# Last token tile: five PSUM banks in turn for its MoE, expert weights split in pieces of 1024 columns, its rows' scale from the bits of the norm on VectorE

## The chip, the cores and the metric

The kernel runs on one core of one Trainium2 chip. The metric is device time in microseconds (us) of one execution, lower is better. Names of engines are those of the profile: PE is TensorE (PEld its weight loads), DVE is VectorE, ACT is ScalarE, POOL is GpSimd, SP is SyncE. "Lo" and "hi" are the two float16 halves into which the kernel splits every float32 matrix so that three float16 products replace one float32 product.

## The reference

Three layers follow one another on 1152 tokens of 512 values.

```
attn:  2 batches x 8 heads x 576 x 64, top_k = 32 of 576 scores kept, softmax, times v
x      = attn as (1152, 512)
moe:   xn = x / sqrt(mean(x*x) + 1e-6) * rms_g
       x  = (silu(xn @ w_gate) * (xn @ w_val)) @ w_out          # 512 -> 1536 -> 512
moe2:  expert = argmax(x @ r_gate, 8 experts); gate_w = softmax of the same logits at that expert
       disp[e, c] = x[i]   in order of i, at most 288 rows for an expert
       y   = relu(disp @ w1[e]) @ w2[e]                         # 512 -> 1024 -> 512
       out[i] = gate_w[i] * y[expert[i], pos[i]]
```

## The kernel before

The 1152 tokens are nine tiles of 128 rows (t = 0 to 8). For each tile, attention runs over four pairs of heads; after it come `norm(t)`, `moe1(t)` (the dense MoE) and `dispatch(t)` (routing, and one indirect DMA that writes the tile's rows to `disp` in HBM). A table of slots (`at(...)`) says when each of these generators takes a step, and a scheduler orders the instructions of each engine from that; the order that results is fixed when the kernel is built. Attention is the largest part of the span (until about 511 us); what follows it is the subject here: tile 7's MoE is half done then, tile 8's MoE still has to run alone, and then the eight experts.

`moe1(t)` has six products `b` = 0 to 5 of twelve matmuls each (128x512), gate and value in turn for three groups g of 512 columns. Each fills one PSUM bank `a` of the pool `pm` (three banks). For tile 8, ACT takes the tanh of a gate product (`th`), DVE makes the gate from it (L456) and multiplies the value product by it (L459, `gs`); only then is a bank free. `turned(g)` transposes the result on PE, also through `pm`, and ACT and DVE make its halves `hT` (L422, L423). The 36 matmuls of the second layer (L473) add up in `yps`, also a bank of `pm`, and ACT copies it out as `yx` (L479).

`dispatch(t)` takes the norm of the rows on ACT (L495), a power of two near its inverse square root on POOL (`pow`, L132 and L133, called from L497) and DVE (L139, L142), scales the rows, finds the expert, and DVE writes the row numbers into `slot` (L554). POOL then issues the scatter (L556). For tile 8 the first gather, of expert 0's first 128 rows ("a"), is issued on ACT's queue (L760, L773) and waits for tile 7's scatter. After tile 8's scatter SP issues the gathers of experts 1 to 3, and of the rest of expert 0 ("b": POOL fetches its rows as `xb`, SP transposes them).

The sixteen expert weights (`w1`, `w2` of eight experts, 2 MB each, loaded as two DMAs of 1 MB) come in the order `ORDER`; below, weight n is the n-th in that order. Each passes through `load` (SP's queue), `size` (two ACT squares of 2048 columns into `junk`, L720, a small PE sum, five small DVE steps) and `convert` (hi half on ACT L744 and on DVE L746, lo half in two DVE pieces L749). Weights 0 and 1 are read from the buffers `split2` and `split3`, the others from `raw` buffers, of which there are two at first and four in the expert stage. A raw buffer is free when its weight's lo half is done. Weights 0 to 3 are sized and converted during tile 8's MoE, weight 4 at its end, weights 5 to 15 in the expert stage. The loads of weights 5, 6 and 7 are issued only after the gather of expert 3 (`issue_after(last.ins)`).

In the expert stage PE alternates `up` and `down` (L832), 96 matmuls each; `up` of expert e needs weight `w1[e]` converted.

## Time and profile before

| | us |
|---|---|
| median of 3 runs | 720.37 (718.26 to 722.33) |
| the profiled execution, device time | 719.72 |
| its span, first to last instruction | 717.9 |
| busy: PE / DVE / ACT / POOL | 557.7 / 625.8 / 493.6 / 423.4 |
| mean granted TensorE clock | 0.933 |

The profile is of one execution; 1.8 us lie around its span. A time such as 571.45 is counted from the span's start. A share of busy time over the whole span says little here, since attention, the dense MoE and the experts have different limits; what counts is who waits for whom after 511 us.

### The profile page before, as it was taken

The page shows a single profiled execution, that of the slowest core. Times are in us where ns is not written, and L with a number is a line of the kernel's source. Part 1 is how long each engine was busy: PE and PEld are TensorE (multiplying, and loading weights), DVE is VectorE, ACT ScalarE, POOL GpSimd, SP SyncE. Part 2 cuts the span into 40 slices and gives each one's busy share as a digit, 9 for nine tenths or more (in the row PEclk, how much of TensorE's full clock was granted, in tenths as well). Part 3 has the DMA queues.
Part 4 walks back from the last instruction along what each step waited for, and adds up shares of the span by engine and source line. Part 5 has one row for each costly group of instructions (what it writes and reads, how often), then busy time and mean ns, then how long its engine had stood idle before and what let it go on. Part 6 is the DMA issues. An engine that isn't in the chain of part 4 may idle for free.

```text
span 717.9 us, 12959 instructions
## 1 busy us (share of the span) xinstructions
PE 557.7 (78%) x4700; PEld 400.0 (56%) x4700; DVE 625.8 (87%) x1296; ACT 493.6 (69%) x939; POOL 423.4 (59%) x446
## 2 busy tenths in 40 slices
PE   1216425476667999999999999998987859999995
PEld 1115314334344666666556565665534549998994
DVE  3999999999999999999999999997389534989960
ACT  3456447559957788878688778877797317998811
POOL 3786888867895778866858767765513220023412
PEclk9999655569999999999999999999999989999998
DMA  8999161385000002000000000000933179999101
GB/s 212 270 320 288 43 211 38 125 248 166 8 8 16 16 22 50 27 12 16 23 16 24 16 15 16 1 16 1 370 114 118 45 203 362 296 328 296 44 21 38
DMA packets 47016, 80.00 MB, mean 111 GB/s; under 512 B 18732, under 2 KB 23340, under 8 KB 46946
## 3 DMA queue, kind: packets, MB, share of 16 engines
q1 hardware_dynamic: 43954, 74.02, 33.7%
q0 software_dynamic: 1792, 4.83, 1.8%
q8 instruction: 39, 0.64, 0.4%
q10 hardware_dynamic: 1200, 0.26, 0.2%
q14 instruction: 31, 0.25, 0.1%
HBM read 64.35 MB, written 12.27 MB: 107 GB/s over the span
## 4 chain that ended last, share of the span: by engine, by line
DVE 49%; issue 15%; PE 11%; ACT 8%; DMA 8%; POOL 6%; SPq 1%; POOLq 0%; ACTq 0%; DVEq 0%
DVE r L333 14%; DVE m L336 14%; DVE m L324 5%; PE pm L448 4%; PE pm L473 3%; DMA raw<-in_w_dram 3%; DVE wbig L157 3%; DMA wbig<-in_w_out_dram 3%; ACT junk L720 2%; DVE wbig L159 2%; DVE wbig L228 2%; POOL out_dram L874 2%; DMA vt<-in_v_l_dram 2%; DVE split L749 1%; DVE hT L423 1%
## 5 line engine op out<-in xcount | busy, mean ns | idle before, releaser
L448 PE MATMUL pm<-wbig,xn 128*128 128x512 f16 x648 | 165.3, 390 | 10.4 <-POOL wbig L225 3.2
L336 DVE MAX8 m<-r 128x8 f32<-128x576 f32 x216 | 157.1, 747 | 0.3
L832 PEld LDWEIGHTS <-split 128*128 128x128 f16 x1728 | 115.2, 99 | 13.1 <-issue 13.0
L310 PE MATMUL tp<-kst,qh 128*128 128x288 f32 (+1 forms) x160 | 64.8, 416 | 64.6 <-ACT s L312 23.8
L353 POOL TENSOR_TENSOR pp<-s,pp 128x576 f32<-128x576 f32 x72 | 102.7, 1442 | 8.6 <-ACT pp L352 8.4
L333 DVE MATCH_REPLACE8 r<-m,r 128x576 f32<-128x576 f32 x144 | 106.5, 742 | 0.0
L448 PEld LDWEIGHTS <-xn 128*128 128x128 f16 x648 | 62.9, 100 | 74.6 <-issue 16.2
L473 PE MATMUL pm<-wbig,hT 128*128 128x512 f16 x324 | 80.9, 388 | 11.9 <-POOL wbig L229 3.1
L310 PEld LDWEIGHTS tp<-kst,qh 128*128 128x128 f32 (+1 forms) x160 | 32.3, 203 | 92.2 <-ACT s L312 31.8
L352 ACT ACTIVATE pp<-s,bias 128x576 f32<-128x576 f32 x72 | 52.0, 773 | 27.9 <-POOL bias L338 27.6
L376 PE MATMUL tp<-ident,pp 128*128 128x128 f32 x324 | 57.9, 295 | 15.8 <-ACT pp L358 7.3
L312 ACT ACTIVATE s<-tp 128x288 f32<-128x288 f32 x144 | 54.8, 412 | 19.3 <-POOL pp L353 15.8
L874 POOL DMA_INDIRECT out_dram<-ob,tos x14 | 23.1, 1647 | 73.8 <-ACT ob L872 71.7
L749 DVE SCALAR_TENSOR_TENSOR split<-raw,sc,split 128x2048 f16<-128x2048 f32 x28 | 65.1, 2344 | 0.3 <-ACT split L744 0.3
L832 PE MATMUL acc<-hE,split 128*128 128x168 f16 (+2 forms) x864 | 58.7, 228 | 2.9 <-DVE hE L843 2.0
L384 PE MATMUL xps<-pt,vt 128*64 128x128 f32 (+1 forms) x800 | 57.9, 284 | 2.9 <-ACT pt L377 2.9
L377 ACT ACTIVATE pt<-tp 128x384 f32<-128x384 f32 x108 | 49.3, 494 | 14.1 <-PE tp L376 11.4
L376 PEld LDWEIGHTS tp<-ident,pp 128*128 128x128 f32 x324 | 41.7, 150 | 30.5 <-ACT pp L358 10.1
L720 ACT ACTIVATE junk<-raw 128x2048 bf16<-128x2048 f32 x28 | 53.4, 1909 | 7.4 <-DMA raw<-in_w_dram 7.2
L832 PE MATMUL acc<-xgT,split 128*128 128x168 f16 (+1 forms) x768 | 56.6, 234 | 2.3 <-DVE yT L851 2.3
L358 ACT ACTIVATE pp<-pp,bias 128x576 f32<-128x576 f32 x72 | 56.4, 785 | 0.1
L473 PEld LDWEIGHTS <-hT 128*128 128x128 f16 x324 | 30.4, 100 | 45.7 <-issue 11.8
(191 smaller groups left out, 1247.3 us busy)
## 6 DMA issues: line engine op xcount, KB each, us to landing
raw<-in_w_dram SPq DMA_DIRECT2D x28, 1024.0 KB, 7.9
wbig<-in_w_out_dram SPq DMA_DIRECT2D x6, 1024.0 KB, 9.9
disp<-wraw SPq DMA_DIRECT2D x18, 257.0 KB, 7.0
qraw<-in_q_l_dram SPq DMA_DIRECT2D x72, 64.0 KB, 2.2
wraw<-in_w_gate_dram SPq DMA_DIRECT2D x8, 512.0 KB, 4.5
split<-in_w_dram SPq DMA_DIRECT2D x4, 1024.0 KB, 7.2
kraw<-in_k_l_dram SPq DMA_DIRECT2D x12, 288.0 KB, 4.3
wbig<-in_w_val_dram SPq DMA_DIRECT2D x3, 1024.0 KB, 6.1
```

What stands on the lines that cost most here:

```text
L310: nc.tensor.matmul(sp[:c1], x[:, i, :c1], kst[b, hp][:, i, c * HALF:(c + 1) * HALF], start=(n == 0), stop=(n == 1))
L333: nc.vector.match_replace(r[i], m[:, i, n - 1], src, -3.0e38)
L336: nc.vector.max(m[:, i, n], r[i])
L353: nc.gpsimd.tensor_tensor(w, s[i], w, op=OP.subtract)
L358: nc.scalar.activation(pp[p][:, i], pp[p][:, i], AF.Exp, bias=bias[:, i, 0:1], scale=0.125, accum_out=sums[t][:, h:h + 1])
L376: nc.tensor.transpose(tp[:, i, :], p2[:, o:o + P], ident)
L384: nc.tensor.matmul(xps[t][rows, hp, c0:c1], v, w, start=(n == 0), stop=(n == 4))
L448: nc.tensor.matmul(a, xn[:, x + c, :], half(i, lo), start=(c == 0 and n == 0), stop=(c == KC - 1 and n == 2))
L473: nc.tensor.matmul(yps, hT[f // KC][:, KC * hi + f % KC, :], half(i, lo), start=(f == 0 and n == 0), stop=(f == NF1 - 1 and n == 2))
L720: nc.scalar.activation(junk, raw[:, g * BIG:(g + 1) * BIG], AF.Square, accum_out=sc[:, 9 + g:10 + g])
L749: nc.vector.scalar_tensor_tensor(lo[:, r], raw[:, r], sc[:, 7:8], hi[:, r], op0=OP.mult, op1=OP.subtract)
L832: nc.tensor.matmul(a, u[:, c, col * P:(col + 1) * P], v[:, c, :a.shape[-1]], start=(c == 0 and n == 0), stop=(c == nk - 1 and n == 2))
```

## The change

Four edits, all for what follows attention. First, when attention's PSUM is given back, a new pool `late` takes two of its banks, and tile 8's products b = 1, 2, 4, 5 use them; b = 0 and 3, the transposes and `yps` stay in `pm`. Tile 8's `moe1` starts at table slot 18 of its stretch and not 12, which is after the pool is made. Second, weights 0 to 3 are squared and converted in four pieces of 1024 columns and not two of 2048 (the first half on ACT, the second on DVE, as before); weights 4 to 15 keep two pieces. Third, tile 8's power of two is worked out on DVE from the bits of the norm, as the expert weights' already is, and POOL's two steps go. Fourth, as a result, the scheduler orders all engines anew from tile 8's MoE on.

```diff
--- before.py
+++ after.py
@@ -424,6 +424,8 @@
 
     yx = {}
 
+    late = []
+
     def moe1(t, ew):
         hT = [mx.tile([P, 2 * KC, P], F16, name="hT", bufs=3) for _ in range(3)]
         xn = xnT.pop(t)
@@ -440,8 +442,8 @@
             if ew is nc.gpsimd:
                 gs = mx.tile([P, DM], F32, name="gs")
             for w in range(2):
-                a = pm.tile([P, DM], F32, name="pm")
                 b = 2 * g + w
+                a = late[0].tile([P, DM], F32, name="late") if late and b % 3 else pm.tile([P, DM], F32, name="pm")
                 for c in range(KC):
                     i = KC * b + c
                     for n, (x, lo) in enumerate(((0, 0), (0, 1), (KC, 0))):
@@ -493,8 +495,8 @@
         nc.gpsimd.tensor_copy(yd[:, DM + 1:ROW], tok[:, t:t + 1])
         yn = route.tile([P, 8], F32, name="yn")
         nc.scalar.activation(yd[:, :DM // 2].bitcast(BF16), y, AF.Square, accum_out=yn[:, 0:1])
-        size = pow2_below_rsqrt(yn[:, 1:2], yn[:, 2:3], yn[:, 0:1], 1.01, yn[:, 3:5])
-        next(size)
+        size = iter(()) if t == NT - 1 else pow2_below_rsqrt(yn[:, 1:2], yn[:, 2:3], yn[:, 0:1], 1.01, yn[:, 3:5])
+        next(size, None)
         yield
         lp = px.tile([P, 3, E], F32, name="px")
         for c in range(KC):
@@ -504,6 +506,13 @@
         nc.vector.tensor_copy(lg, lp[:, 0, :])
         for _ in size:
             pass
+        if t == NT - 1:
+            nc.vector.tensor_scalar(yn[:, 3:4], yn[:, 0:1], 1.1, TINY, op0=OP.mult, op1=OP.add)
+            bits = yn[:, 4:5].bitcast(I32)
+            nc.vector.tensor_scalar(bits, yn[:, 3:4].bitcast(I32), 1, 0x7fff0000, op0=OP.logical_shift_right, op1=OP.bitwise_and)
+            nc.vector.tensor_scalar(bits, bits, -1, 0x5f370000, op0=OP.mult, op1=OP.add)
+            exponent(yn[:, 1:2], yn[:, 4:5])
+            invert(yn[:, 2:3], yn[:, 1:2])
         nc.vector.tensor_scalar(yn[:, 5:6], yn[:, 1:2], YS, None, op0=OP.mult)
         if t == NT - 1:
             nc.scalar.activation(yh, y, AF.Copy, scale=yn[:, 5:6])
@@ -646,7 +655,7 @@
         ew = nc.vector if t in (0, 8) else nc.gpsimd
         t0 = (4 * t + 5) * SL
         at(t0 + 1, ahead(norm(t, ew), 300), 1)
-        at(t0 + 12, ahead(moe1(t, ew), 0), 2.7)
+        at(t0 + (12 if t < NT - 1 else 18), ahead(moe1(t, ew), 0), 2.7)
         at(t0 + 10 + 4 * SL, ahead(dispatch(t), 0), 3 if t < NT - 1 else 1)
     live = []
     slot = 0
@@ -675,6 +684,7 @@
     ps.release()
     ew = ctx.enter_context(tc.tile_pool(name="ew", bufs=1, reuse_waits="tile"))
     pst = ctx.enter_context(tc.tile_pool(name="pst", bufs=1, space=PSUM, side="right", reuse_waits="tile"))
+    late.append(tc.alloc_tile_pool(name="late", bufs=2, space=PSUM, side="right"))
     slots = [ew.tile([P, 8 * DM], F32, name=f"split{i}") for i in range(4)]
     raws = [ew.tile([P, 8 * DM], F32, name=f"raw{i}") for i in range(2)]
     es = {}
@@ -715,14 +725,15 @@
         e, w = divmod(j, 2)
         raw = raw_of(n)
         sc = ew.tile([P, 13], F32, name="sc", bufs=8)
-        for g in range(2):
-            junk = ew.tile([P, BIG], BF16, name="junk")
-            nc.scalar.activation(junk, raw[:, g * BIG:(g + 1) * BIG], AF.Square, accum_out=sc[:, 9 + g:10 + g])
+        k = 4 if n < 4 else 2
+        for g in range(k):
+            junk = ew.tile([P, BIG], BF16, name="junk")[:, :2 * BIG // k]
+            nc.scalar.activation(junk, raw[:, g * 2 * BIG // k:(g + 1) * 2 * BIG // k], AF.Square, accum_out=sc[:, 9 + g:10 + g])
         t = pst.tile([P, DM], F32, name="st")
-        s16 = ew.tile([P, 2], BF16, name="s16", bufs=2)
-        nc.vector.tensor_copy(s16, sc[:, 9:11])
-        for g in range(2):
-            nc.tensor.matmul(t[:, 0:1], ones16, s16[:, g:g + 1], start=(g == 0), stop=(g == 1))
+        s16 = ew.tile([P, 4], BF16, name="s16", bufs=2)
+        nc.vector.tensor_copy(s16[:, :k], sc[:, 9:9 + k])
+        for g in range(k):
+            nc.tensor.matmul(t[:, 0:1], ones16, s16[:, g:g + 1], start=(g == 0), stop=(g == k - 1))
         nc.vector.tensor_scalar(sc[:, 2:3], t[:, 0:1], 1.01, TINY, op0=OP.mult, op1=OP.add)
         half_bits = sc[:, 3:4].bitcast(I32)
         nc.vector.tensor_scalar(half_bits, sc[:, 2:3].bitcast(I32), 1, 0x7fff0000, op0=OP.logical_shift_right, op1=OP.bitwise_and)
@@ -738,14 +749,15 @@
     def convert(j, n):
 
         raw, (hi, lo), sc = raw_of(n), place(j), sized.pop(j)
-        for g in range(2):
-            r = slice(g * BIG, (g + 1) * BIG)
-            if g == 0:
+        k = 4 if n < 4 else 2
+        for g in range(k):
+            r = slice(g * 2 * BIG // k, (g + 1) * 2 * BIG // k)
+            if 2 * g < k:
                 nc.scalar.activation(hi[:, r], raw[:, r], AF.Copy, scale=sc[:, 7:8])
             else:
                 nc.vector.tensor_scalar(hi[:, r], raw[:, r], sc[:, 7:8], None, op0=OP.mult)
-        for g in range(2):
-            r = slice(g * BIG, (g + 1) * BIG)
+        for g in range(k):
+            r = slice(g * 2 * BIG // k, (g + 1) * 2 * BIG // k)
             nc.vector.scalar_tensor_tensor(lo[:, r], raw[:, r], sc[:, 7:8], hi[:, r], op0=OP.mult, op1=OP.subtract)
 
     meta, every, xgT, hE, yT2 = {}, {}, {}, {}, {}
@@ -788,6 +800,7 @@
         fetch_w()
     while live or fill:
         advance()
+    late.pop().release()
     px.release()
     pm.release()
     wts.release()
```

The new order is shown at three places. Line numbers of the changed kernel are its own: L457 to L461 there are L455 to L459 before, L731 is L720, L756 is L744, L758 is L746, L761 is L749, L718 is L708.

DVE before, from the third weight's hi half to tile 8's last gate (`th` is a gate, `gs` a value product, `sc` the small steps of a weight's size, `split` with a number is a weight's converted buffer):

```order
L746 TENSOR_SCALAR split_5660<-raw_5662,sc 128x2048
L527 MAX k_5704<-key 128x8
L735 TENSOR_TENSOR sc<-sc 128x1
L749 SCALAR_TENSOR_TENSOR split_5660<-raw_5662,sc,split_5660 128x2048
L530 TENSOR_SCALAR oh<-rank_72,k_5704 128x8
L749 SCALAR_TENSOR_TENSOR split_5660<-raw_5662,sc,split_5660 128x2048
L539 TENSOR_SCALAR nm<-nm 128x1
L456 SCALAR_TENSOR_TENSOR th<-th,pm 128x512
L538 SCALAR_TENSOR_TENSOR scr,pos<-first,oh 128x8
```

DVE of the change, from tile 8's last gate to its last `hT`:

```order
L458 SCALAR_TENSOR_TENSOR th<-th,late 128x512
L739 TENSOR_SCALAR sc<-sc 128x1
L423 TENSOR_TENSOR hT<-pm,hT 128x512
L461 SCALAR_TENSOR_TENSOR gs<-late,st,th 128x512
...
L761 SCALAR_TENSOR_TENSOR split_5636<-raw_5638,sc,split_5636 128x1024 x2
L739 TENSOR_SCALAR sc<-sc 128x1
L761 SCALAR_TENSOR_TENSOR split_5636<-raw_5638,sc,split_5636 128x1024
L548 TENSOR_SCALAR nm<-nm 128x1
L539 TENSOR_SCALAR oh<-rank_72,k_5684 128x8
L423 TENSOR_TENSOR hT<-pm,hT 128x512
```

Before, the last gate stood behind the whole conversion of weights 2 and 3 (`split_5660` is weight 3's); now it stands ahead of both, and the last `hT` stands behind weight 2's (`split_5636`).

ACT before, around the copy of tile 8's result `yx`:

```order
L720 ACTIVATE junk,sc<-raw_5661 128x2048
L760 DMA_TRANSPOSE xgT<-disp 128x8x128
L773 DMA notes_5885<-disp 128x2
L422 ACTIVATE hT<-pm 128x512
L479 ACTIVATE yx<-pm,st 128x512
L744 ACTIVATE split_5988<-raw_5661,sc 128x2048
L495 ACTIVATE yd,yn<-yx 128x512
```

ACT of the change, the same place:

```order
L481 ACTIVATE yx<-pm,st 128x512
L731 ACTIVATE junk,sc<-raw_5638 128x2048
L492 ACTIVATE xu<-px 128x512
L772 DMA_TRANSPOSE xgT<-disp 128x8x128
L785 DMA notes_5889<-disp 128x2
L497 ACTIVATE yd,yn<-yx 128x512
L731 ACTIVATE junk,sc<-raw_5638 128x2048
```

The gather "a" and its notes moved from ahead of `yx` to between `yx` and tile 8's norm (L497), and weight 4's squares (`raw_5638`) moved behind `yx`.

SP before, its DMAs from weight 4's load on (each row is one weight's two DMAs; `raw_5661` twice is weights 4 and 8, `raw_5662`, `raw_5989` and `raw_5990` below the gathers are weights 5, 6, 7):

```order
L708 DMA raw_5661<-in_w_dram 128x2x1024 x2
L708 DMA raw_5661<-in_w_dram 128x4x512 x2
L760 DMA_TRANSPOSE xgT<-disp 128x8x176
...
L760 DMA_TRANSPOSE xgT<-disp 128x8x176
L708 DMA raw_5662<-in_w_dram 128x2x1024 x2
L708 DMA raw_5989<-in_w_dram 128x4x512 x2
L708 DMA raw_5990<-in_w_dram 128x2x1024 x2
```

SP of the change:

```order
L718 DMA raw_5638<-in_w_dram 128x2x1024 x2
L772 DMA_TRANSPOSE xgT<-disp 128x8x176
...
L772 DMA_TRANSPOSE xgT<-disp 128x8x176
L718 DMA raw_5639<-in_w_dram 128x2x1024 x2
L718 DMA raw_6034<-in_w_dram 128x4x512 x2
L718 DMA raw_6035<-in_w_dram 128x2x1024 x2
L718 DMA raw_5638<-in_w_dram 128x4x512 x2
```

Weight 8's load moved from ahead of the gathers to behind weight 7's load, and with it weight 4's conversion, which frees its buffer: on DVE that now stands behind tile 8's scatter.

## Rows read from the trace of the kernel before

**Rows 1.** Windows: length; busy us of PE, PEld, DVE, ACT, POOL; clock; DMA share; GB/s.
```profile
526.00:568.00 42.00, 33.50 (x157) 15.69 (x155) 33.27 (x67) 27.26 (x34) 7.72 (x8) 0.92 0.19 64
580.00:600.00 20.00, 12.48 (x224) 12.22 (x222) 2.98 (x10) 3.66 (x5) 2.40 (x3) 0.83 0.84 237
600.00:710.00 110.00, 104.31 (x1454) 101.67 (x1451) 87.52 (x140) 79.13 (x88) 22.07 (x13) 1.00 0.66 197
```

**Rows 2.** Timeline of PE in tile 8's MoE: start, us, instruction, [idle before <-releaser].
```profile
529.67 4.02 PE L448 MATMUL pm<-wbig,xn 128*128 128x512 f16 x10
...
539.66 2.75 PE L448 MATMUL pm<-wbig,xn 128*128 128x512 f16 x12 [1.19 <-DVE th L456]
...
548.19 2.75 PE L448 MATMUL pm<-wbig,xn 128*128 128x512 f16 x12 [1.44 <-DVE th L456]
...
556.69 7.03 PE L473 MATMUL pm<-wbig,hT 128*128 128x512 f16 x24 [2.69 <-DVE th L456]
```

**Rows 3.** Timeline of ACT and DVE in the same stretch.
```profile
528.36 0.60 ACT L422 ACTIVATE hT<-pm 128x512 f16<-128x512 f32 x1
...
531.86 0.69 DVE L423 TENSOR_TENSOR hT<-pm,hT 128x512 f16<-128x512 f32 x1
...
557.40 0.73 DVE L459 SCALAR_TENSOR_TENSOR gs<-pm,st,th 128x512 f32<-128x512 f32 x1
```

**Rows 4.** Timeline: tile 8's result, norm, power of two and slots.
```profile
568.17 0.69 ACT L479 ACTIVATE yx<-pm,st 128x512 f32<-128x512 f32 x1 [3.27 <-PE pm L473]
...
570.65 0.62 ACT L495 ACTIVATE yd<-yx 128x512 bf16<-128x512 f32 x1
...
571.98 2.56 POOL L133 TENSOR_TENSOR yn<-yn,mhalf 128x1 f32<-128x1 f32 x1
...
574.57 0.15 DVE L139 TENSOR_SCALAR yn<-yn 128x1 int32<-128x1 int32 x1 [0.47 <-POOL yn L133]
...
578.38 0.15 DVE L554 TENSOR_TENSOR slot<-pos 128x1 int32<-128x1 f32 x1
```

**Rows 5.** Timeline: tile 7's slots, scatter, and the gather "a" on ACT's queue.
```profile
558.37 0.16 DVE L554 TENSOR_TENSOR slot<-pos 128x1 int32<-128x1 f32 x1
...
562.26 1.36 ACTq L760 DMA_TRANSPOSE xgT<-disp  x1
...
563.65 0.60 ACTq L773 DMA_DIRECT2D notes<-disp  x1
```

**Rows 6.** Chain of waits behind tile 8's scatter: start, us, what.
```profile
583.16 4.99 DMA xb<-disp,rest
```

**Rows 7.** Timeline: loads on SP's queue, and PE's first matmul behind the gathers.
```profile
571.90 2.59 SPq L708 DMA_DIRECT2D raw<-in_w_dram  x2
...
590.90 6.56 SPq L708 DMA_DIRECT2D raw<-in_w_dram  x6
591.06 4.00 PE L832 MATMUL acc<-xbT,split 128*128 128x48 f16 x96 [6.68 <-DMA xbT<-xb]
```

**Rows 8.** Timeline: weight 4's lo half on DVE, a later load, the last lo half.
```profile
569.49 4.61 DVE L749 SCALAR_TENSOR_TENSOR split<-raw,sc,split 128x2048 f16<-128x2048 f32 x2
...
610.53 2.03 SPq L708 DMA_DIRECT2D raw<-in_w_dram  x2
...
685.75 4.61 DVE L749 SCALAR_TENSOR_TENSOR split<-raw,sc,split 128x2048 f16<-128x2048 f32 x2
```

**Rows 9.** The page's groups for a weight's lo piece and square: busy, mean ns.
```profile
L749 DVE SCALAR_TENSOR_TENSOR split<-raw,sc,split 128x2048 f16<-128x2048 f32 x28 | 65.1, 2344 | 0.3 <-ACT split L744 0.3
...
L720 ACT ACTIVATE junk<-raw 128x2048 bf16<-128x2048 f32 x28 | 53.4, 1909 | 7.4 <-DMA raw<-in_w_dram 7.2
```

**Rows 10.** Timeline: two of POOL's scatters of results, and DVE beside the first.
```profile
630.65 2.34 DVE L749 SCALAR_TENSOR_TENSOR split<-raw,sc,split 128x2048 f16<-128x2048 f32 x1
...
631.05 2.80 POOL L874 DMA_INDIRECT out_dram<-ob,tos  x1 [15.55 <-ACT ob L872]
...
695.43 0.93 POOL L874 DMA_INDIRECT out_dram<-ob,tos  x1 [0.30 <-issue]
```

## The prediction

> **What bounds the kernel now.** The change touches nothing ahead of tile 8's MoE, so I read the windows behind attention first. The windows [rows 1] show three stretches. In 526 to 568, tile 8's MoE runs alone: PE is busy 33.5 of 42 us, and part of that at the lower of its two clock levels (granted 0.92 of 2.4 GHz on the mean). In 580 to 600, between tile 8's scatter and the experts, every engine idles: DVE is busy 3.0 of 20 us, ACT 3.7. In 600 to 710 PE is busy 104.3 of 110 us at full clock, DVE 87.5, ACT 79.1: the experts run at PE's pace. So the end moves with the moment at which PE may start on the gathered rows, 591.06, where it had waited 6.68 us for the last transposed gather [rows 7]. The chain of waits shows what stands there: the fetch of `xb`, 4.99 us, behind tile 8's scatter [rows 6]. The scatter follows `slot`, which DVE writes at 578.38 [rows 4]. Hence the question is how much earlier `slot` comes.
>
> Back from `slot`, PE's timeline [rows 2] shows tile 8's MoE waiting for a PSUM bank three times, 1.19, 1.44 and 2.69 us, each time for DVE's gate (L456), and ten matmuls at 0.40 us each (4.02 us) where twelve later ones took 2.75, that is 0.22. The last gate was late because DVE had two weights to convert first; the last `gs` came at 557.40 [rows 3]. The result was copied out at 568.17 and its norm taken at 570.65; POOL's `pow` then took 2.56 us, and DVE could go on at 574.57 [rows 4].
>
> **The change, step by step.** A price first. A piece of 1024 columns does not occur before. A lo piece lies between half of 2.34 [rows 9], 1.17, and a third of the way from 0.69 for 512 columns [rows 3] to 2.34, which is 1.24; I take 1.22. A square lies between half of 1.91 and a third of the way from 0.62 [rows 4] to 1.91, 0.95 to 1.05; I take 1.05. Four weights have eight squares and four hi pieces more on ACT, and four hi and eight lo pieces more on DVE, each at most 0.19 and 0.14 dearer: at most 2.3 us on ACT and 1.7 on DVE over 45 us, nothing below. They count where the engine is the bound.
>
> 1. *Start.* Tile 7's `hT` on ACT was at 528.36 [rows 3], behind four squares of 2048 columns and a hi half. Now six squares of 1024 stand ahead of it and the hi pieces behind: about 2 us earlier, 526.3; it can't be the whole 3.9 saved, because PE's transposes have to come first. DVE's `hT`, at 531.86, comes about 2.8 earlier. PE's idle time there shrinks to under 1 us, so I expect full clock.
>
> 2. *PE's run.* With five banks PE needs no gate until product b = 4. From 526.3 it has 72 matmuls of the first layer and tile 7's last 12: 84 at 0.22 are 18.5, with 1.7 for transposes and sums 546.5. Before, it was through with these by 556 or somewhat earlier: 5.3 us of bank waits and 1.8 at the lower clock (ten times 0.18) are gone, and the start is 2 earlier.
>
> 3. *DVE takes over as the bound.* In the new order the last `hT` of tile 8 stands behind weight 1's and weight 2's lo pieces. PE comes to weight 1's sum behind 48 of its matmuls (526.3 and 10.6, 536.9), and with five small steps (0.9) and two hi pieces (1.4) DVE is at 539.2. From there it has to do without a gap: six steps of 512 columns at 0.7 (4.2), eight lo pieces at 1.22 (9.8), two hi pieces (1.4), some twenty small steps at about 0.1 (2.0): 17.4, so the last `hT` stands at 556.6 to 557.3. PE is idle for 3 us by then, so its last ten matmuls take 2.2 to 4.0; I take 3.6, because ten behind such a wait were at 0.40 [rows 2]. `yx` is copied at 561.0 instead of 568.17: 7.2 earlier.
>
> 4. *ACT gives 2.8 back.* Before, 2.48 lay between `yx` and the norm [rows 4]. Now a square (1.91), a copy (0.6) and the issue of gather "a" and its notes stand there (1.36 and 0.60 [rows 5]), which ACT did before while it was idle. 561.0 with 0.65, 1.9, 0.6 and 2.0 is 566.2. The gather also waits for tile 7's scatter. DVE writes tile 7's `slot` behind the last `hT`, nine small steps (1.2) and two hi pieces (1.4): 560.1, later than the 558.37 of before; the scatter took 3.73 from there to the gather's issue [rows 5]: 563.9, while ACT is there at 564.2. If POOL is held up by a lo piece, 0.9 is lost; I take 0.3. The norm's sum is there at 567.2 instead of 571.3: 4.1 earlier.
>
> 5. *The bits on DVE.* From the norm's sum to the exponent took 3.3 (to 574.57 [rows 4]). Now it is three small steps of 0.19, but in DVE's order the cast of the notes of "a" stands among them and waits until they land. Landing takes something between nothing and the 3.7 of a scatter; I take 2 from the end of the issue (566.5), 568.5. Exponent at 569.1: 5.5 earlier.
>
> 6. *Tail.* From there to `slot` it was 3.8 [rows 4], with two lo halves of `hE` (0.7 each) in between, which now stand behind: 2.4 to 3.8, I take 3.3. `slot` at 572.4 instead of 578.4: **6.0 earlier**.
>
> 7. *What is moved into the expert stage.* Weight 4's conversion (4.61 for its lo half [rows 8], some 7 with hi half and sizes) stood beside tile 8's end; it now runs behind tile 8's scatter, in order behind a cast that waits for `xb`. It is free because DVE idles 17 of those 20 us [rows 1]; without that cover it is 7. Its buffer's next load, weight 8's, was issued at 571.90 and now goes behind weights 5 to 7, whose issue begins at 590.90 less 6 [rows 7]. This too should cost nothing: the load after those, at 610.53, had to wait for a buffer to be converted, not for the queue [rows 8], so there is a gap for 2 MB.
>
> The sum is made against the profiled execution: 719.72 less 6.0 is 713.7. It is 0.65 below the median of the runs, so on the median's footing 720.37 less 6.0, **714.4 us**. About 0.5% is what a measurement of this kernel can tell from no change.
>
> **A rule and a row on POOL.** While DVE ran a lo half from 630.65 on, a scatter of POOL's that started at 631.05 took 2.80, where undisturbed ones took 0.93 [rows 10]; it ended 0.86 behind the lo half, so it was held for one DVE instruction. The Trainium skill, SBUF — State Buffer, section Who interferes with whom, says that a DVE instruction with two SBUF inputs contends with a GpSimd instruction that reads SBUF, and that the second one blocks until the first finishes. By that rule, the trace agrees, a piece of 1024 holds tile 7's scatter for 1.2 at most; but four such pieces stand in a row there, and the rule does not say that POOL gets in between them.
>
> **Rivals.**
>
> *POOL gets in only behind all four pieces* (chance 0.18). Place: tile 7's scatter, beside weight 3's four lo pieces. Price 4.9: gather at 568.8, norm at 571.5, no gain so far; notes at 572.8, exponent 573.4, `slot` 576.7, 1.7 earlier: 718.7. Against it: the scatter that began at 631.05 was held by one instruction only. It also stands for a DVE that is some 4 us slower on its pieces than I think.
>
> *More gain* (0.16). Steps 4 to 6 at their low ends: no hold, notes landed when the cast comes, `hE` fully out of the way: 0.3, 1.4 and 0.9 more, 8.6 in all: 711.8.
>
> *The expert stage runs at the loader's pace, not PE's* (0.12), which ends on the other side. Weights 5 to 15 took from 590.90 to 690.4, the end of the last lo half [rows 7, 8], 99.5 us for eleven, 9.0 each; PE needs 7.2 matmul time for a weight's 96 products and little more. If the loop of load, squares, conversion and free buffer sets the pace, weight 4's conversion and weight 8's load add one step to it: 720.4 less 6.0 and 9.0 more, 723.4, and if conversion and load cost a step each, one behind the other, 732. It decides from the point where weight 5's conversion, at about 598 now, starts later than its data by more than a us or so. For it: DVE is busy 87.5 of 110 us there. Against it: PE is busy 104.3 of them.
>
> **How the numbers follow.** Forecast 0.54 (712.5 to 716.8), more gain 0.16, POOL held 0.18, loader 0.12. Faster by over 0.5% (below 716.8) is the first two, 0.70; slower (above 724) is two thirds of the last, 0.08; the rest is within 0.5%, 0.22. The range leaves out some 0.08 at each end: 710.0 to 722.0, wide enough for the bounds of step 3 to 6 on both sides.
>
> **What would show it.** Right: PE without bank waits on L458 and at full clock until b = 5; the last `gs` near 549, the last `hT` near 557, `yx` near 561, the norm near 566.5, `slot` near 572.4; first matmul on `xbT` near 585, and 600 to 710 as full of PE as before but 6 earlier. Wrong: the gather "a" issued after 566, DVE's cast of the notes waiting past 569.5, or PE waiting for converted weights between experts; a PE gap there of over 2 us refutes step 7.

## The result, and the profile after

The changed kernel takes 709.27 us, the kernel before 720.55 beside it (medians of four runs each): a ratio of 0.985, 95% interval 0.982 to 0.988. A second measurement gave 710.74 and 0.985 (0.981 to 0.989). So it is faster by 1.5%, some 11 us, where 6.0 were forecast: the direction and the place were right, the time lies 5 us below the forecast and 0.7 us outside the range, whose lower end is 710.0; the second measurement lies 0.7 inside it.

The profiled execution has a span of 707.2 us against 717.9. Its windows answer to [rows 1]:

```profile
526.00:568.00 42.00, 33.13 (x188) 18.60 (x186) 35.28 (x85) 32.18 (x52) 6.32 (x8) 0.91 0.19 64
580.00:600.00 20.00, 16.43 (x351) 16.21 (x349) 12.89 (x22) 11.71 (x13) 1.03 (x1) 1.00 0.99 340
590.00:700.00 110.00, 103.59 (x1461) 101.76 (x1458) 88.76 (x145) 81.06 (x92) 20.95 (x15) 1.00 0.70 224
```

The stretch from 580 on, where every engine had idled, is now work at full clock (granted 1.00 where 0.83 stood). The experts, 10 us earlier, fill PE as before: 103.6 of 110 us.

PE's timeline answers to [rows 2, 7]: no product waits for a gate, and the first matmul on `xbT` comes 8.6 us earlier and takes 2.60 us instead of 4.00.

```profile
542.03 2.75 PE L450 MATMUL late<-wbig,xn 128*128 128x512 f16 x12
...
555.50 2.33 PE L475 MATMUL pm<-wbig,hT 128*128 128x512 f16 x10 [0.41 <-DVE sc L740]
...
582.43 2.60 PE L845 MATMUL acc<-xbT,split 128*128 128x48 f16 x96 [2.30 <-DMA xbT<-xb]
...
593.89 0.19 PE L736 MATMUL st<-s,ones 128*128 128x1 bf16 x2 [1.27 <-DVE s L734]
```

DVE, the bound of tile 8's MoE, answers to [rows 3 to 5]: last `gs`, last `hT`, tile 7's `slot`, weight 3's four lo pieces, and from 565.41 on the bits of the norm.

```profile
547.03 0.74 DVE L461 SCALAR_TENSOR_TENSOR gs<-late,st,th 128x512 f32<-128x512 f32 x1
...
554.76 0.68 DVE L423 TENSOR_TENSOR hT<-pm,hT 128x512 f16<-128x512 f32 x1
...
557.35 0.15 DVE L563 TENSOR_TENSOR slot<-pos 128x1 int32<-128x1 f32 x1
...
557.49 4.87 DVE L761 SCALAR_TENSOR_TENSOR split<-raw,sc,split 128x1024 f16<-128x1024 f32 x4
...
565.41 0.15 DVE L510 TENSOR_SCALAR yn<-yn 128x1 f32<-128x1 f32 x1 [3.05 <-ACT yd L497]
566.32 0.15 DVE L872 CAST to<-notes 128x1 int32<-128x1 f32 x1 [0.76 <-PE px L503]
...
566.75 0.15 DVE L139 TENSOR_SCALAR yn<-yn 128x1 int32<-128x1 int32 x1
...
570.15 0.15 DVE L563 TENSOR_TENSOR slot<-pos 128x1 int32<-128x1 f32 x1
```

ACT, POOL and SP between the two `slot`s: behind `yx` a wait that nobody foresaw, 3.25 us for weight 4's data; the gather "a" behind tile 7's scatter, for whose end POOL waits 2.86 us; the norm behind that.

```profile
525.24 0.59 ACT L422 ACTIVATE hT<-pm 128x512 f16<-128x512 f32 x1
...
557.93 0.67 ACT L481 ACTIVATE yx<-pm,st 128x512 f32<-128x512 f32 x1
...
558.30 1.43 POOL L565 DMA_INDIRECT disp<-yd,slot  x1 [2.92 <-DVE sc L746]
...
561.85 1.91 ACT L731 ACTIVATE junk<-raw 128x2048 bf16<-128x2048 f32 x1 [3.25 <-DMA raw<-in_w_dram]
...
562.56 1.36 ACTq L772 DMA_TRANSPOSE xgT<-disp  x1
...
562.60 0.18 POOL L495 COPY yd<-tok 128x1 f32<-128x1 f32 x1 [2.86 <-DMA disp<-yd,slot]
...
564.65 0.63 ACT L497 ACTIVATE yd<-yx 128x512 bf16<-128x512 f32 x1 [0.32 <-ACT xu L492]
...
574.05 1.52 SPq L772 DMA_TRANSPOSE xgT<-disp  x1
```

To compare profiles, I count from the start of ACT's first square of weight 0, which lies between 513.17 and 517.18 in the fourteen profiles here, since attention ahead of it varies. "Up b" is PE's work on `xbT`; "scatter t8" is POOL's start of tile 8's scatter; "stage" is from the first matmul of expert 1's `up` (up 1) to the end of the span. "After" stands twice, for its two profiles.

| kernel | first square | norm | scatter t8 | up b | idle before it | up b takes | up 1 | end | stage | time, ratio |
|---|---|---|---|---|---|---|---|---|---|---|
| before | 515.57 | 55.08 | 63.74 | 75.49 | 6.68 | 4.00 | 79.31 | 202.33 | 123.02 | 720.55 |
| after | 515.39 | 49.26 | 55.78 | 67.04 | 2.30 | 2.60 | 69.47 | 191.81 | 122.34 | 709.27, 0.985 |
| after, again | 517.13 | 49.14 | 55.65 | 67.48 | 2.28 | 2.60 | 69.91 | 192.87 | 122.96 | 710.74, 0.985 |
| no banks | 514.86 | 52.12 | 58.74 | 70.44 | 4.03 | 3.74 | 74.02 | 195.44 | 121.42 | 714.16, 0.991 |
| no pieces | 514.85 | 57.82 | 67.84 | 79.48 | 4.10 | 3.75 | 83.53 | 215.15 | 131.62 | 729.57, 1.011 |
| no bits | 513.61 | 49.16 | 55.59 | 66.86 | 2.37 | 2.60 | 69.30 | 192.39 | 123.09 | 708.97, 0.983 |
| no pieces, weight 4 late | 514.90 | 56.41 | 61.66 | 73.80 | 1.95 | 2.59 | 76.23 | 198.60 | 122.37 | 715.22, 0.993 |
| before, weight 4 late | 513.17 | 53.12 | 60.63 | 72.29 | 4.02 | 3.85 | 75.98 | 198.93 | 122.95 | 715.87, 0.995 |

Some expectations below have stage and end 400 too high (523 for 123, 591.8 for 191.8), a slip in a subtraction; their differences hold.

### The profile page after: what moved, and what is told of

The parts are those of the page before. It is cut to its first block, busy times and chain, and to the rows that moved or that the text cites. A ratio compares the mean times of both kernels' runs of the same rounds, so it can differ in the third digit from the quotient of the medians.

```text
span 707.2 us, 13015 instructions
## 1 busy us (share of the span) xinstructions
PE 555.5 (79%) x4708; PEld 401.9 (57%) x4708; DVE 627.0 (89%) x1311; ACT 495.8 (70%) x959; POOL 414.9 (59%) x444
## 3 DMA queue, kind: packets, MB, share of 16 engines
q1 hardware_dynamic: 43954, 74.02, 33.2%
## 4 chain that ended last, share of the span: by engine, by line
DVE 49%; issue 16%; PE 11%; ACT 8%; DMA 8%; POOL 6%; SPq 1%; POOLq 0%; ACTq 0%; DVEq 0%
DVE r L333 14%; DVE m L336 14%; DVE m L324 5%; PE pm L450 4%; DMA wbig<-in_w_out_dram 3%; DVE wbig L157 3%; ACT junk L731 3%; DMA raw<-in_w_dram 3%; POOL out_dram L887 2%; DVE wbig L159 2%; DVE split L761 2%; DVE wbig L228 2%; DMA vt<-in_v_l_dram 2%; PE pm L475 2%; DVE hT L423 1%
## 5 line engine op out<-in xcount | busy, mean ns | idle before, releaser
L450 PE MATMUL pm<-wbig,xn 128*128 128x512 f16 x600 | 152.1, 387 | 8.8 <-POOL wbig L225 3.2
L475 PE MATMUL pm<-wbig,hT 128*128 128x512 f16 x324 | 79.1, 383 | 7.7 <-POOL wbig L229 3.7
L761 DVE SCALAR_TENSOR_TENSOR split<-raw,sc,split 128x2048 f16<-128x2048 f32 (+1 forms) x32 | 65.8, 2078 | 0.1
L887 POOL DMA_INDIRECT out_dram<-ob,tos x14 | 20.2, 1445 | 73.8 <-ACT ob L885 58.4
L731 ACT ACTIVATE junk<-raw 128x2048 bf16<-128x2048 f32 (+1 forms) x32 | 54.2, 1693 | 9.9 <-DMA raw<-in_w_dram 9.5
L324 DVE MAX8 m<-s 128x8 f32<-128x576 f32 x72 | 53.6, 745 | 0.0
```

Source lines behind the costliest of these rows:

```text
L324: nc.vector.max(m[:, i, 0], s[i])
L450: nc.tensor.matmul(a, xn[:, x + c, :], half(i, lo), start=(c == 0 and n == 0), stop=(c == KC - 1 and n == 2))
L475: nc.tensor.matmul(yps, hT[f // KC][:, KC * hi + f % KC, :], half(i, lo), start=(f == 0 and n == 0), stop=(f == NF1 - 1 and n == 2))
L731: nc.scalar.activation(junk, raw[:, g * 2 * BIG // k:(g + 1) * 2 * BIG // k], AF.Square, accum_out=sc[:, 9 + g:10 + g])
L761: nc.vector.scalar_tensor_tensor(lo[:, r], raw[:, r], sc[:, 7:8], hi[:, r], op0=OP.mult, op1=OP.subtract)
```

## The experiments

**Each edit undone by itself.** Without the extra banks, `late` isn't made and `b` stays in `pm`:

```diff
-    late.append(tc.alloc_tile_pool(name="late", bufs=2, space=PSUM, side="right"))
```

> The changed kernel without the two extra PSUM banks: all six products of tile 8 take their bank from pm again; pieces, bits on VectorE and slot 18 stay. Theory A (the end follows the start of PE on xbT, and the banks free PE and DVE in tile 8's MoE): PE waits for gates again, 1 us or more each, the last gs comes 3 to 6 us later than the 547.0 of the changed kernel, yx near 561.5 to 564 instead of 557.9, and the end moves by about as much, 711 to 714 us in all. Rival (the pieces and the new order of DVE do it, the banks little): yx within 1.5 us of 557.9, time within 1.5 us of the changed kernel's 709.3.

Ratio 0.991 (0.988 to 0.994), 714.16 us, as theory A had it: norm 2.9 and scatter 3.0 later than after, up 1 4.6 later, the end 3.6. PE waits for DVE again, 1.57 and 1.27 us, and 12 matmuls behind that take 4.45 us where [rows 2] have 2.75:

```profile
544.98 0.66 PE L436 MATMUL pm<-ident,gs 128*128 128x128 f32 x4 [1.57 <-DVE sc L736]
...
546.91 4.45 PE L450 MATMUL pm<-wbig,xn 128*128 128x512 f16 x12 [1.27 <-DVE sc L738]
```

The idle time ahead of up b is 4.03 us here and up b takes 3.74, so 1.1 of the 4.6 us at up 1 are up b's length. The pieces without the banks, with weight 4's move that comes with them (below) and with the bits, thus give 6.9 of the 10.5 us between before and after.

> The changed kernel with all weights squared and converted in two pieces of 2048 columns, as before; banks and bits stay. Weight 4 is then squared and converted ahead of tile 8's end again, and weight 8's load comes early again. Theory A (only the path to slot counts, the expert stage runs at PE's pace): the last gs and the last hT stand behind more conversion on DVE, yx near 562 to 564, slot near 574 to 576 instead of 570.15, and the end later by the same 4 to 6 us: 713 to 715 us. Rival (the conversion of weight 4 moved into the expert stage has a price or a gain of its own there): the stretch from PE's first matmul on xbT to the end differs by 2 us or more from that of the changed kernel (582.43 to 707.2, 124.8), and the time doesn't follow slot.

```diff
-        k = 4 if n < 4 else 2
+        k = 2
```

729.57 us, ratio 1.011 (1.005 to 1.017): 20 us above the changed kernel and slower than before. Neither theory had that; the rival's sign is there (the stretch from PE's first matmul on `xbT` to the end takes 135.7 us instead of 124.8), but not for its reason. The timeline of PE and DVE shows three places where the time goes.

```profile
551.83 2.59 DVE L761 SCALAR_TENSOR_TENSOR split<-raw,sc,split 128x2048 f16<-128x2048 f32 x1
...
554.42 2.33 DVE L761 SCALAR_TENSOR_TENSOR split<-raw,sc,split 128x2048 f16<-128x2048 f32 x1
...
556.74 1.27 DVE L423 TENSOR_TENSOR hT<-pm,hT 128x512 f16<-128x512 f32 x2
...
557.47 7.38 PE L475 MATMUL pm<-wbig,hT 128*128 128x512 f16 x20 [4.35 <-DVE hT L423]
...
567.55 4.61 DVE L761 SCALAR_TENSOR_TENSOR split<-raw,sc,split 128x2048 f16<-128x2048 f32 x2
...
577.98 0.15 DVE L872 CAST to<-notes 128x1 int32<-128x1 f32 x1 [4.39 <-DMA notes<-disp]
...
680.19 4.61 DVE L761 SCALAR_TENSOR_TENSOR split<-raw,sc,split 128x2048 f16<-128x2048 f32 x2
...
684.78 2.35 DVE L761 SCALAR_TENSOR_TENSOR split<-raw,sc,split 128x2048 f16<-128x2048 f32 x1
...
687.04 1.68 DVE L856 SCALAR_TENSOR_TENSOR hE<-acc,hE 128x504 f16<-128x504 f32 x3
...
687.77 9.66 PE L845 MATMUL acc<-hE,split 128*128 128x168 f16 x96 [7.02 <-DVE hE L856]
```

Tile 8's last two `hT` stand behind weight 3's lo half, so PE idles 4.35 us and does 20 matmuls at 0.37 us. Weight 4's lo half and weight 8's load are back beside the dispatch, and the cast of the notes, ahead of the bits, waits 4.39 us. And in the expert stage three `hE` pieces stand behind a run of four lo pieces in DVE's order: 7.02 us of idle PE, then 96 matmuls in 9.66 us where the changed kernel has 7.12. That is the stage of 131.6 in the table.

> The changed kernel with tile 8's power of two taken from POOL's pow again; banks and pieces stay. Norm of tile 8 near 564.7 as in the changed kernel; pow puts its exponent at about 568.0 to 568.7 instead of 566.75, slot near 572 and PE's first matmul on xbT near 584.4, behind an idle time of about 4.2 us instead of 2.3 (6.7 before). Theory A (PE's clock falls in a long enough idle time and up b pays for it): up b takes about 4.0 instead of 2.60 and the time is 3.3 us longer, 712.6. Rival (the length of up b has nothing to do with the idle time, or 4.2 us are not enough): up b 2.6 and the time 1.9 us longer, 711.2.

```diff
-        size = iter(()) if t == NT - 1 else pow2_below_rsqrt(...)
+        size = pow2_below_rsqrt(...)
...
-        if t == NT - 1:                # and the steps on the bits under it
```

708.97 us, ratio 0.983 (0.977 to 0.989): no loss at all, where both theories had one; on the clock the run decides nothing, since the idle time stayed at 2.37 us and up b at 2.60. `pow` takes 0.57 us here, not the 2.56 of [rows 4], and is through before the cast of the notes is, which stands ahead of the exponent:

```profile
563.85 0.57 POOL L133 TENSOR_TENSOR yn<-yn,mhalf 128x1 f32<-128x1 f32 x1
...
564.49 0.15 DVE L865 CAST to<-notes 128x1 int32<-128x1 f32 x1 [3.92 <-DMA notes<-disp]
564.56 0.14 DVE L139 TENSOR_SCALAR yn<-yn 128x1 int32<-128x1 int32 x1
```

**Weight 4 moved out of the way, by itself.** In the changed kernel weight 4's conversion left tile 8's end without an edit that says so. Here it is moved alone, in the kernel before and in the one without pieces; `ends` holds tile 8's last step on ACT and its `slot` on DVE:

```diff
-        convert(ORDER[n], n)
+        with tc.issue_after(ends["act"].ins), tc.issue_after(ends["dve"].ins):    # n == 4, size(ORDER[4], 4) likewise
+            convert(ORDER[n], n)
```

> Banks and bits with weights in two pieces of 2048 columns as in the run without pieces, but with all of weight 4's squares and conversion put behind tile 8's slot, where the changed kernel has them too. Theory A (the pieces count because they let hT of tile 8 get in between the lo halves on DVE): yx stays near 565, where the run without pieces had it, the dispatch behind it gets 2 to 5 us shorter, 724 to 728 us. Rival (the pieces count because weight 4's conversion and weight 8's load left tile 8's end with them): most of the 20 us come back, 711 to 716 us.

715.22 us, 0.993 (0.990 to 0.996): the rival was right on the time, 14 of the 20 us come back. `yx` stays at 565.42, as theory A said, but the scatter comes 6.2 earlier, and the new order of the expert stage has no stall of 7 us; that part is 9.2.

> The kernel before with one thing moved and nothing else: weight 4's squares and conversion stand behind tile 8's slot on ACT and DVE, as they do in the changed kernel (weight 8's load then moves behind weights 5 to 7 by itself, since it needs weight 4's buffer). Theory A (part of the 10.7 us is this move, which is no edit of the change but follows from it): no lo half of weight 4 beside POOL's pow, which then takes about 0.6 instead of 2.56; no hi half of 2 us ahead of the norm; slot 3.5 to 4 us earlier against the first square, and the last DMA of the scatter lands sooner (3.9 instead of 4.58 from slot to SP's first gather); 715.5 to 717 us. Rival (the move has a price in the expert stage, where conversion and loads have no room): the stretch from up 1 to the end is 2 us or more longer than the 523.0 of before less the start of the first square, and the time is 719 us or more.

715.87 us, ratio 0.995 (0.992 to 0.999); in the profile the end is 3.4 us earlier at a stage of 122.95, against 123.02. So theory A held in the main: the move alone is worth about a third of the gain (1 to 6 us by the interval) and costs nothing later. The norm is 2.0 and `slot` 3.1 earlier, where 3.5 to 4 were expected for `slot`. `pow` takes 0.57 us:

```profile
567.38 0.57 POOL L133 TENSOR_TENSOR yn<-yn,mhalf 128x1 f32<-128x1 f32 x1
...
576.84 1.52 SPq L761 DMA_TRANSPOSE xgT<-disp  x1
...
585.46 3.85 PE L833 MATMUL acc<-xbT,split 128*128 128x48 f16 x96 [4.02 <-DMA xbT<-xb]
```

From `slot` (572.86) to SP's first gather it takes 3.98 us, against 4.58 before. That weight 8's load, which ran beside the scatter before, is the reason is not shown: the two kernels below that keep this load where it was take 4.03 and 4.07. Nor does it reach PE, since up b starts 3.2 us earlier, as `slot` does.

**The clock of up b.** Matmuls that nobody reads are put between `down("a")` and `up("b")` of the kernel before, 96 and then 144:

```diff
     down("a", 0, WA)
+    filler = pacc.tile([P, DM], F32, name="acc")
+    for c in range(KC):
+        product(filler[:, c * P:(c + 1) * P], place(1), hE["a"], NF2, DM, c)
```

> The kernel before with 96 matmuls of 128 columns more between down a and up b, whose result nobody reads: PE then has work for some 5 us of the 6.68 in which it waited for xbT. Theory A (up b took 4.00 instead of 2.60 because PE stood idle before it and was granted the lower clock): up b takes about 2.6, starts as before at 591.1, up 1 starts 1.4 us earlier at 593.5, and added work makes the kernel no slower, up to 1.4 us faster, if the new order of the expert stage costs nothing. Rival (up b was slow because of the eight weight loads that run beside it): up b stays near 4.0 and nothing gets earlier.

> The kernel before with 144 matmuls of 128 columns more between down a and up b (the run with 96 left 2.75 us without work). They take 8.2 us, so that PE works until xbT is there, 591 or the same less the run's offset. Theory A (the lower clock of up b comes from the idle time ahead of it): granted clock 1.00 throughout, up b 2.6 instead of 4.00, up 1 starts 1.4 us earlier against the start of the weights' first square. Rival (the loads beside it): up b 3.5 to 4.0 again, at 0.50.

For 144, a second such tile of two columns of 128 follows. With 96 PE still idled 2.75 us and up b took 3.51, which is neither theory's time; it begins at the higher level, which falls within the first of these windows, and the second, inside up b, has the lower one:

```profile
589.30:591.00 1.70, 1.70 (x55) 1.69 (x55) 0.00 (x0) 0.00 (x0) 0.00 (x0) 0.76 0.87 182
591.00:592.70 1.70, 1.70 (x47) 1.70 (x45) 0.00 (x0) 0.00 (x0) 0.00 (x0) 0.50 1.07 325
```

With 144 it takes 2.60 at a granted clock of 1.00, with loads beside it as before; theory A is right on up b and the rival falls. Up 1 starts 78.59 behind the first square instead of 79.31, 0.7 earlier and not 1.4, since up b came 0.2 later and four transposes now stand between the two.

```profile
589.24 2.60 PE L832 MATMUL acc<-xbT,split 128*128 128x48 f16 x96 [1.17 <-DMA xbT<-xb]
...
601.77 0.19 PE L725 MATMUL st<-s,ones 128*128 128x1 bf16 x2 [2.68 <-DVE s L723]
```

Neither was faster: 720.08 us (0.999, 0.996 to 1.003) and 725.40 (1.006, 1.003 to 1.010). The second row shows why for the larger one: the filler made the scheduler order the expert stage anew, with waits of 2.68, 3.16 and 2.73 us on PE, and the stage takes 131.25.

**Can the remaining waits be had?** Four versions of the changed kernel, each taking away a wait that the one before still has.

> The changed kernel with the two squares of weight 4 put behind tile 8's norm on ACT (in the changed kernel the first of them stands behind yx and waits 3.25 us for its data, with the norm behind it). Theory A (that wait costs nothing, because the issue of gather a stands ahead of the norm too and waits for tile 7's scatter until 562.5 anyway): norm near 564.5 as in the changed kernel (564.65), up b near 582.4, time within 1.5 us of 709.3. Rival (the wait for weight 4 is what holds the norm): norm at 561 to 562, slot about 2 to 3 us earlier, 706 to 707 us.

```diff
-            size(ORDER[4], 4)
+            with tc.issue_after(norms[-1].ins):
+                size(ORDER[4], 4)
```

710.80 us, 0.987 (0.982 to 0.991). Theory A: the norm comes 48.92 behind the first square, 0.3 earlier. The 3.25 us wait held nothing that the gather's issue didn't hold as well.

> The changed kernel with everything taken away from ahead of tile 8's norm and slot that they do not need: gather a and its notes are issued on SP's queue, which is empty there, weight 4's squares stand behind ACT's last step for tile 8, and the casts of the notes and of weight 4's squares behind slot on DVE. Theory A: norm near 560.3 instead of 564.65; DVE comes to it behind weight 3's lo pieces, at 562.4, slot near 567 instead of 570.15, and then PE's own up a and down a, which end near 580.1, set the start of up b (582.43 in the changed kernel): 2.3 us at most are gained, about 707 us. Rival (the later squares of weight 4 delay its conversion and with it down of expert 1, or gather a is late on SP): PE waits in the expert stage, time 709 us or more.

```diff
-            gather("a", 0, 0, WA, ew, nc.scalar)
+            gather("a", 0, 0, WA, ew, nc.sync)
...
-    send("a", WA, True)
+    with tc.issue_after(ends["dve"].ins):
+        send("a", WA, True)
```

708.50 us, 0.983 (0.979 to 0.988), no gain against the changed kernel. The norm is 1.9 earlier, not 4: it writes its squares into `yd`, which tile 7's scatter still reads. And the product for the rows' positions stands on PE behind 26 matmuls of `up("a")`:

```profile
562.00 0.63 ACT L498 ACTIVATE yd<-yx 128x512 bf16<-128x512 f32 x1 [1.51 <-DMA disp<-yd,slot]
...
565.18 2.93 PE L846 MATMUL acc<-xgT,split 128*128 128x128 f16 x26 [1.58 <-DMA xgT<-disp]
...
567.91 0.21 PE L543 MATMUL px<-oh,before 128*128 128x8 bf16 x1
```

> The kernel with gather a on SP's queue and weight 4's squares late, and two more waits taken away that it showed: tile 8's norm writes its squares into another buffer than the rows that tile 7's scatter still reads (it waited 1.51 us for it), and up a stands behind the two small products for the rows' positions on PE (they stood behind 26 of its matmuls, which waited for the gathered rows); casts that wait for DMAs stand behind. Theory A (PE's chain to slot is then free, and PE's own up a and down a are the bound): norm 0.5 us behind yx, slot 3 to 3.5 us earlier than in the run before (54.0 behind the first square), up b behind down a with under 0.5 us of idle time, some 2 us earlier; 706 to 707.5 us. Rival (another wait takes their place, xbT or weight 5 in the expert stage): up b not earlier than 66.5 behind the first square, or the stretch from up 1 to the end grows by what is gained; 708.5 us or more.

```diff
+        sq = mx.tile([P, DM], F32, name="gs") if t == NT - 1 else yd
...
-    up("a", 0, WA)
+    with tc.issue_after(ends["pe"].ins):
+        up("a", 0, WA)
```

709.12 us, 0.986 (0.982 to 0.991). Half of theory A came true: up b starts behind `down("a")` without any idle time, 65.02 behind the first square, 2.0 earlier. The rival took it back: PE waits 3.74 us for weight 5's squares, and the stage takes 124.28. Up a, which now is part of the bound, takes 8.19 us for its 96 matmuls at a granted clock of 0.50 for the most part, behind waits of PE; before, it took 5.7.

```profile
567.96 8.19 PE L847 MATMUL acc<-xgT,split 128*128 128x128 f16 x96 [1.92 <-DMA xgT<-disp]
...
582.20 2.59 PE L847 MATMUL acc<-xbT,split 128*128 128x48 f16 x96
...
594.16 0.19 PE L738 MATMUL st<-s,ones 128*128 128x1 bf16 x2 [3.74 <-DVE s L736]
```

> The kernel of the run before, in which up b started 2 us earlier but PE then waited 3.74 us for the squares of weight 5, with weight 5's load issued behind the notes of a (its raw buffer is free since weight 3's lo half is done) and no longer behind the gather of expert 3; its squares stand behind hE of a. Theory A (the load of weight 5, which follows the last gather, is the next bound at the entry to the expert stage): the wait of 3.74 us goes, the stretch from up 1 to the end falls from 524.3 back to 522 or less, 704 to 706 us. Rival (2 MB beside tile 8's scatter and gathers delay these by as much): up b 2 us later or more than 65.0 behind the first square, 708 us or more.

```diff
+    with tc.issue_after(ends["notes", "a"].ins):
+        fetch_w()
     with tc.issue_after(last.ins):
-        for _ in range(3):
+        for _ in range(2):
             fetch_w()
...
+            with tc.issue_after(ends["h", "a"].ins), tc.issue_after(ends["a"].ins):
+                size(ORDER[n + 1], n + 1)
```

710.43 us, 0.984 (0.980 to 0.988): the rival. The wait for weight 5 is down to 0.51, but its 2 MB run beside tile 8's scatter, whose end POOL awaits 4.84 us instead of 2.21, and up b starts 2.3 later. Another wait takes the place of the first, too: PE waits 4.04 us for a `hE` piece that DVE does behind a lo half, and the stage takes 125.31.

```profile
574.76 0.97 POOL L830 DMA_INDIRECT xb<-disp,rest  x1 [4.84 <-DMA disp<-yd,slot]
...
583.05 2.60 PE L847 MATMUL acc<-xbT,split 128*128 128x48 f16 x96 [2.47 <-DMA xbT<-xb]
...
597.81 1.12 PE L847 MATMUL acc<-hE,split 128*128 128x48 f16 x24 [4.04 <-DVE hE L858]
```

> The changed kernel itself once more, on the chip and beside the runs of the kernel of this call. Both theories: 709.3 us within 1 us, up b near 67.0 and the end near 591.8 behind the start of the first square, as in the profile of after.

710.74 us, 1.4 above the first measurement and so outside the expected 1 us; up b at 67.48 and the end at 192.87 are 0.4 and 1.1 later than in the first profile, so a single profile, and each "end" above, is good to about 1 us. No version beats the changed kernel by more.

## Why the prediction was right, and where it failed

What it said of the mechanism held in the main: PE is free of bank waits, DVE bounds tile 8's MoE, the expert stage keeps its pace. What failed is the size of step 4 and the sum behind it. Step 4 put tile 7's `slot` at 560.1 and with it the norm 4.1 us earlier; `slot` came at 557.35 and the norm 5.8 to 5.9 earlier. The sum then let the end move by just the 6.0 of `slot`, and so kept up b at its 4.00 us of before without a reason; it took 2.60, 1.4 us more. With the 2.1 us by which `slot` came earlier than forecast, 714.4 would have been 712.3, with the 1.4 of up b 713.0, and with both 710.9; what is left is within the 1 us by which two profiles of the changed kernel differ. The shift against before, counted from the first square, step by step:

| moment | forecast | after | after, again |
|---|---|---|---|
| `yx` | -7.2 | -10.1 | -8.8 |
| norm | -4.1 | -5.8 | -5.9 |
| exponent | -5.5 | -7.6 | -7.7 |
| `slot` | -6.0 | -8.1 | -8.2 |
| up b starts | -6.0 | -8.5 | -8.0 |
| up 1 starts | -6.0 | -9.8 | -9.4 |
| end | -6.0 | -10.5 | -9.5 |

1. *Start and PE's run (steps 1 and 2)*: right, 1 to 2 us too cautious. ACT's `hT` at 525.24, forecast 526.3; the last first-layer product ended at 544.8, forecast 546.5 for all of it.

2. *DVE as the bound (step 3)*: the chain has its forecast length, 17.2 us from 538.20 to the end of the last `hT` at 555.44 (forecast 17.4), but starts 1.0 earlier. The last ten matmuls were priced at 3.6 us: 2.33 in the first profile, 3.70 in the second (the ten of [rows 2] at 0.40 stood behind 1.61 us of idle PE, not behind 3). This term moves `yx` and nothing else, because the norm comes at 49.26 and 49.14.

3. *ACT gives back (step 4)*: this is the first mis-sized term. What sets the norm is tile 7's `slot`, then its scatter, then the gather's issue. `Slot` was forecast for 560.1 and came at 557.35: the 1.0 from the start, and 1.9 us behind the last `hT` where 2.6 were put, on top of an `hT` taken at its late end. Of these 2.75 us, 1.0 was lost again, which step 4 did not have: POOL waits 2.86 us for the scatter's end where it waited 1.88 before. Weight 4's load still lands then (ACT waits for it until 561.85); that it is the cause was not tested.

```profile
562.30 0.18 POOL L493 COPY yd<-tok 128x1 f32<-128x1 f32 x1 [1.88 <-DMA disp<-yd,slot]
```

The hold on POOL was 0.34 (1.43 against 1.09), forecast 0.3, so POOL does get in between two lo pieces, and the rival that it waits behind all four falls. The unforeseen 3.25 us wait cost 0.3 at most.

4. *The bits (step 5)*: the exponent came 2.1 us earlier than forecast, of which 1.7 stand at the norm already; the cause of the gain was wrong. POOL's `pow` took 2.56 us in [rows 4] because weight 4's lo half ran on DVE beside it [rows 8]; without that it takes 0.57, and the kernel is as fast with it. The prediction weighed that very effect on tile 7's scatter and did not see it in the row of `pow`, so the gain of this step, 1.4 us forecast and 1.8 measured, came out nearly right by luck: with `pow` left in place it comes as well, from weight 4's move. The Trainium skill, SBUF — State Buffer, section Who interferes with whom, says that GpSimd's SBUF ports are shared with DVE and locked by one of them at a time; 2.56 against 0.57 agrees.

5. *Tail (step 6)*: right, 3.4 against 3.3.

6. *What is moved into the expert stage (step 7)*: "costs nothing" held, as the stage lasted 122.3 and 123.0 against 123.0. But the move was counted as a possible cost only. By itself it brings 3.4 us: 2.0 stand at the norm, ahead of which a hi half less stands on ACT, and 3.1 at `slot`, with `pow` in between.

7. *The term that was missing*: up b itself. The 4.00 us of [rows 7] were taken as its length, while the window 591 to 593 of before has it at a granted clock of 0.50, after 6.68 us of idle PE. At 2.3 us of idle time PE keeps 1.00, and up b takes 2.60: 1.4 us. In the table it took 2.59 to 2.60 behind 2.37 us of idle time or less, and 3.74 to 4.00 behind 4.02 to 6.68. Two profiles lie between and differ: 2.60 behind 2.83 us (weight 4's squares late), 3.51 behind 2.75 (96 extra matmuls). The Trainium skill, TensorE: Matmul & The Clock Gate, section HAM oscillation — how this bites in real kernels, describes waits for DMAs after which the next stretch begins at the low clock; up b of before (4.00 us at 0.50) and the run with 144 extra matmuls (2.60 at 1.00) agree, while with 96 (3.51) the clock fell only inside up b. The lower level has not left the changed kernel: after 5.08 us of idle PE, up a runs at 0.50 there for the most part and takes 8.0 us for 96 matmuls where it took 5.7 before. It costs nothing there, since PE waits 2.30 us for `xbT` all the same; where up b followed without idle time (8.19 us for up a) it did, and no run filled that gap.

Of the 4.5 us between forecast and first profile, 2.1 are steps 3 to 5, 0.4 the stretch from `slot` to up b, 1.4 the clock of up b, and 0.7 the stage; the second profile has 2.2 and 1.4 of these and shows neither the 0.4 nor the 0.7. The rival of more gain came nearer to the time, 711.8, but not by its terms: the hold was there (0.34), the tail was no shorter (3.4), and the notes brought some 0.4 of its 1.4 us. The loader's pace as a rival did not happen in the changed kernel; that the stage can lose 8 to 9 us by its order alone was seen in two others and is not in the prediction at all.

By parts, from the ends: weight 4's move alone 3.4 us, the pieces without banks 6.9, banks and bits without pieces but with the move 3.7, all together 9.5 to 10.5, the bits nothing. The parts don't add up; without pieces, banks and bits made the kernel slower. The banks pay only beside the pieces: 3.6 us there (195.44 to 191.81), 0.3 without them (198.93 to 198.60, with weight 4 late in both), which is less than two profiles of one kernel differ by. What banks alone or pieces alone would give without bits was not run.

## What to carry to other kernels

Before a step is priced from a row, look at what ran beside it and at the clock it was granted: two rows here (`pow` at 2.56, up b at 4.00) were symptoms of work that the change moved. What a change moves without saying so may be worth more than what it edits; undo the parts one by one and move the silent part alone. Where a scheduler orders the queues, any edit upstream is also a new draw for the stages behind it: compare them by their own length.

## What the runs showed of the hardware

Work that serves nothing can shorten what follows it: 144 extra matmuls brought up b from 4.00 to 2.60 us at a granted clock of 1.00 instead of 0.50, though the kernel as a whole got no faster by it. A small step on POOL (`pow`, 128x1) took 2.56 us beside a DVE lo half and 0.57 without; the issue of a scatter beside four lo pieces in a row took 1.43 instead of 1.09, so it got in between them. One load of 2 MB beside a scatter doubled the wait for its end, from 2.2 to 4.8 us.
